# Second queue for the late loads, a new emission order and float32 for the first pairs, in a fused linear-attention and feed-forward kernel

## The chip, the cores and the metric

The kernel runs on one core of one Trainium2 chip. The metric is the device time of one execution in microseconds, median of several runs; the profile is of one such execution. TensorE is called PE in the rows, VectorE DVE, ScalarE ACT, GpSimd POOL, and the queue of SyncE, which issues the transfers, SP or SPq.

## The reference

```python
def phi(x):                                       # S1, S2: (8, 32)
    a = np.einsum('rd,bhsd->bhsr', S1, x)
    b = np.einsum('rd,bhsd->bhsr', S2, x)
    return np.einsum('bhsi,bhsj->bhsij', a, b).reshape(*x.shape[:-1], 64)
q_p, k_p = phi(q), phi(k)                         # q, k, v: (4, 4, 1088, 32)
kv = np.einsum('bhsf,bhsd->bhfd', k_p, v)
z = np.sum(k_p, axis=2)
num = np.einsum('bhsf,bhfd->bhsd', q_p, kv)
den = np.einsum('bhsf,bhf->bhs', q_p, z)[..., None] + 1e-06
x = (num / den).transpose(0, 2, 1, 3).reshape(4352, 128)
h = np.maximum(x @ w_in, 0.0)                     # w_in: (128, 2048)
out = (s * (h * h) + b) @ w_out                   # w_out: (2048, 128)
```

## The kernel before, in words

The 4352 tokens are cut into nine tiles: tile 0 has 256 of them, tiles 1 to 8 have 512. A batch is 1088 tokens, so a tile may need the attention states of two batches. `kvphase(b)` builds the state of one batch: `load_k` and `load_v` bring K and V in three groups of 128-row chunks, `kgroup` makes the features (matmuls L219, a copy `bk` on ACT, two products `ph` on DVE), L249 accumulates them with V, and L272 spreads the sums into `kv_st[b]` with the selection matrix, which lies in the small constant tile `cst_sb`. `first_features` and `first_attend` then make the attention output `x0` of tile 0; `qfeatures(t)` and `qattend(t)` make that of the others, in which the features are spread over the partitions by eight small transfers (`pq`, `br`, L385 and L389) and the denominators by five more (`dc`, `rd`, `rr`).

The feed-forward part goes by eight pairs of 128 hidden columns for each tile (`first_ffn` for tile 0, `ffn` for the others): a first product into `hp`, Relu and Square on ACT, and a second product that accumulates into `ops`. For speed at float32 precision nearly all products are three fp32r matmuls: an operand is cut into a high part (a cast to fp32r, `xh`, `uh`, `wih`, `woh`) and a low part (a subtraction on DVE, `xl`, `ul`, `wil`, `wol`), and high by low, low by high and high by high are added. `product` (L502) issues the three. The weights arrive as 64-bit numbers in eight pieces of 512 KB, `Lw0` to `Lw7`; piece 2i+k is quarter i of `w_in` (k = 0) or of `w_out` (k = 1). `split_weights` makes of a piece the float32 tile `w24` (two steps on ACT, `wc_m` L133 and L149, and two on DVE, L152 and L136), then its high and low parts. Quarter i serves pairs 2i and 2i+1.

Every part is a generator, and the string `ORDER` names, step by step, which one goes on. That fixes the order of instructions within each engine's queue; an engine runs its queue strictly in that order, and each instruction waits for the data and the buffers that it needs. `ON_DVE` lists which casts and copies go to DVE rather than to ACT (the second letter group is tile and pair: `u42` is `uh` of tile 4, pair 2). `SPLIT_0` lists the pairs of tile 0 whose first product, and those whose second product, go by three fp32r matmuls; the others use one float32 matmul with `w24` and the unsplit operand. Buffers are rotated: five for K tiles, five for V tiles, three for queries, four for each of the two kinds of raw weights (the first kind also for the split queries). All transfers are issued from SP. `keep_warm` (z in `ORDER`) is a matmul on constants without a reader.

Of the kernel before, what the change touches and what calls it, by code (L numbers as in the profile page):

```python
# [61 lines left out]
def attn_ffn_kernel(ctx: ExitStack, tc: tile.TileContext, qT, kT, vp, s64, cst, w_in, w_out, outT):  # L62
    nc = tc.nc
# [21 lines left out]

    k_in, v_in = {}, {}

    def load_k(b):
        for g in groups[b]:
            kt = p5.tile([P, GROUP * P], F32, name="kt")  # L90
            nc.sync.dma_start(out=kt[:, :len(g) * P], in_=kT[:, g[0] * P:(g[-1] + 1) * P])  # L91
# [19 lines left out]
    def load_weights(i, k):  # L111
        c = slice(i * CW, (i + 1) * CW)
        raw = p4.tile([P, 2 * CW], I32, name=f"raw{k}")
        nc.sync.dma_start(out=raw, in_=(w_in, w_out)[k][:, c].bitcast(I32))
# [40 lines left out]
    def copy(key, out, in_):  # L155
        (nc.vector.tensor_copy if key in ON_DVE else nc.scalar.copy)(out=out, in_=in_)  # L156

# [131 lines left out]
    def split_x(t, x):  # L289
        N = tiles[t][1] - tiles[t][0]  # L290
        xh = p2.tile([P, NMAX], F32R, name="xh")
        xl = p2.tile([P, NMAX], F32R, name="xl")
# [2 lines left out]
        nc.vector.tensor_tensor(out=xl[:, :N], in0=x[:, :N], in1=f32(xh[:, :N]), op=ALU.subtract)  # L295
# [195 lines left out]
    def split_u(key, u, N):  # L491
        uh = p3.tile([P, 2, NMAX], F32R, name="uh")
        copy(key, uh[:, :, :N], u[:, :, :N])
        yield
# [1 line left out]
        nc.vector.tensor_tensor(out=ul[:, :, :N], in0=u[:, :, :N], in1=f32(uh[:, :, :N]), op=ALU.subtract)  # L496
# [161 lines left out]
```

## Time and profile before

| | |
|---|---|
| median of 3 runs | 251.34 us (250.73, 251.34, 253.22) |
| time of the profiled execution | 250.91 us |
| its span, first to last instruction | 248.7 us |
| PE busy | 237.7 us (96%) |
| ACT busy | 201.9 us (81%) |
| DVE busy | 193.2 us (78%) |
| POOL busy | 1.5 us (1%) |
| moved by DMA | 24.55 MB, 24.30 MB of it on one queue |

A busy PE is not PE at its peak, since the ends of its matmuls are modelled and overlap the next one. The starts are exact, so distances from start to start tell what a matmul costs. Rows of the timeline read: start, duration, engine, line, operation, output and inputs, partitions by elements, count, and in brackets how long the engine had been idle and what ended that.

### The profile page before, as it was taken

The page shows a single profiled execution, that of the slowest core. Times are in us where ns is not written, and L with a number is a line of the kernel's source. Part 1 is how long each engine was busy: PE and PEld are TensorE (multiplying, and loading weights), DVE is VectorE, ACT ScalarE, POOL GpSimd, SP SyncE. Part 2 cuts the span into 40 slices and gives each one's busy share as a digit, 9 for nine tenths or more (in the row PEclk, how much of TensorE's full clock was granted, in tenths as well). Part 3 has the DMA queues.
Part 4 walks back from the last instruction along what each step waited for, and adds up shares of the span by engine and source line. Part 5 has one row for each costly group of instructions (what it writes and reads, how often), then busy time and mean ns, then how long its engine had stood idle before and what let it go on. Part 6 is the DMA issues. An engine that isn't in the chain of part 4 may idle for free.

```text
span 248.7 us, 3985 instructions
## 1 busy us (share of the span) xinstructions
PE 237.7 (96%) x1481; PEld 194.2 (78%) x1482; DVE 193.2 (78%) x269; ACT 201.9 (81%) x266; POOL 1.5 (1%) x10
## 2 busy tenths in 40 slices
...
GB/s 214 346 401 214 205 271 146 224 173 140 146 124 32 211 14 0 143 119 71 100 43 43 108 108 0 0 45 17 69 1 0 17 72 43 0 0 3 42 0 43
DMA packets 16259, 24.55 MB, mean 99 GB/s; under 512 B 4336, under 2 KB 8176, under 8 KB 16240
## 3 DMA queue, kind: packets, MB, share of 16 engines
q1 hardware_dynamic: 16240, 24.30, 33.8%
...
## 4 chain that ended last, share of the span: by engine, by line
PE 89%; DMA 4%; SPq 4%; ACT 1%; issue 1%; DVE 1%; ACTq 0%
PE hp L502 37%; PE ops L502 36%; PE psa L416 4%; DMA raw<-w_in 2%; PE ops L249 2%; PE psa L376 2%; PE psa L502 2%; DMA kt<-kT 2%; SPq L389 2%; PE hp L306 1%; PE psa L219 1%; PE psa L272 1%; SPq L91 1%; SPq L105 1%; PE hp L592 0%
## 5 line engine op out<-in xcount | busy, mean ns | idle before, releaser
L496 DVE TENSOR_TENSOR ul<-u,uh 128x1024 fp32r<-128x1024 f32 (+1 forms) x72 | 83.4, 1162 | 13.0 <-ACT uh L156 11.8
L486 ACT ACTIVATE u<-hp 128x1024 f32<-128x1024 f32 (+1 forms) x72 | 70.3, 976 | 21.5 <-PE hp L502 12.4
L488 ACT ACTIVATE u<-u 128x1024 f32<-128x1024 f32 (+1 forms) x72 | 72.7, 1014 | 1.7
L502 PE MATMUL hp<-xh,wil 128*128 128x512 f32 (+1 forms) x144 | 56.4, 392 | 0.6 <-ACT xh L156 0.6
L502 PE MATMUL hp<-xl,wih 128*128 128x512 f32 (+1 forms) x144 | 55.5, 385 | 0.2 <-DVE xl L295 0.2
L502 PE MATMUL hp<-xh,wih 128*128 128x512 f32 (+1 forms) x144 | 55.2, 384 | 0.0
L502 PE MATMUL ops<-uh,wol 128*128 128x512 f32 (+2 forms) x144 | 53.8, 374 | 0.4 <-ACT kr L156 0.4
L502 PE MATMUL ops<-ul,woh 128*128 128x512 f32 (+2 forms) x144 | 53.4, 371 | 0.0
L502 PE MATMUL ops<-uh,woh 128*128 128x512 f32 (+2 forms) x144 | 53.2, 370 | 0.0
L156 DVE CAST uh<-u 128x1024 fp32r<-128x1024 f32 x43 | 29.7, 691 | 24.3 <-ACT u L488 17.5
L502 PEld LDWEIGHTS hp<-xh,wil 128*128 128x128 f32 x144 | 27.3, 190 | 7.0 <-ACT xh L156 0.7
L502 PEld LDWEIGHTS hp<-xl,wih 128*128 128x128 f32 x144 | 27.4, 190 | 6.1 <-DVE xl L295 0.4
L502 PEld LDWEIGHTS hp<-xh,wih 128*128 128x128 f32 x144 | 27.4, 190 | 5.8
L502 PEld LDWEIGHTS ops<-uh,wol 128*128 128x128 f32 x144 | 27.1, 188 | 5.9 <-ACT kr L156 0.6
L502 PEld LDWEIGHTS ops<-ul,woh 128*128 128x128 f32 x144 | 27.1, 188 | 5.3
L502 PEld LDWEIGHTS ops<-uh,woh 128*128 128x128 f32 x144 | 27.1, 188 | 5.0
L156 ACT CAST uh<-u 128x1024 fp32r<-128x1024 f32 (+1 forms) x29 | 27.0, 933 | 4.2 <-PE ops L502 3.6
L229 DVE TENSOR_TENSOR ph<-psa,bk 128x384 f32<-128x384 f32 x24 | 12.7, 551 | 3.2 <-ACT bk L156 3.1
L219 PE MATMUL psa<-sk,kt 128*64 128x64 f32 x144 | 7.3, 248 | 5.2 <-DVE sk L136 4.3
L219 PEld LDWEIGHTS psa<-sk,kt 128*64 128x64 f32 x144 | 6.1, 159 | 7.1 <-DVE sk L136 5.2
L133 ACT ACTIVATE wc_m<-raw 128x512 f32<-128x512 f32 x8 | 5.4, 673 | 7.4 <-DMA raw<-w_in 4.0
L249 PE MATMUL ops<-ph,vt 128*33 128x64 f32 x288 | 10.9, 229 | 0.5 <-DMA vt<-vp 0.5
...
## 6 DMA issues: line engine op xcount, KB each, us to landing
...
kt<-kT SPq DMA_DIRECT2D x12, 192.0 KB
raw<-w_in SPq DMA_DIRECT2D x4, 512.0 KB
raw<-w_out SPq DMA_DIRECT2D x4, 512.0 KB
...
```

The lines of the kernel that those rows point to most:

```text
L133: nc.scalar.activation(out=out, in_=high.bitcast(F32), func=AF.Abs, scale=2.0 ** -112)
L156: (nc.vector.tensor_copy if key in ON_DVE else nc.scalar.copy)(out=out, in_=in_)
L219: nc.tensor.matmul(av[h:h + 64, :, i, :], kt[:, i * P + h:i * P + h + 64], sk.rearrange("p (w x) -> p w x", w=2), start=(i == 0), stop=(i ...
L229: nc.vector.tensor_tensor(out=ph[:, :n, :, :, j, :].rearrange("p c a i x -> p (c a) i x"), in0=a[:, :n * 32].rearrange("p (g y) -> p g y", ...
L249: nc.tensor.matmul(kvp[0][j * 64:j * 64 + VW, p * 64:(p + 1) * 64].rearrange("q (i x) -> q i x", i=R), v_in[g0][:, l, 2 * p + j], ph[:, l, ...
L376: nc.tensor.matmul(ab[:, :N], w, x[:, :N], start=(i == 0), stop=(i == len(terms) - 1))
L389: nc.sync.dma_start(out=br[d:d + m, p, :N], in_=abs_[32 + 48 * p:32 + 48 * p + m, :N])
L416: nc.tensor.matmul(ps[:, e0:e1], w[:, p, :], x[:, p, e0:e1], start=(i == 0), stop=(i == len(terms) - 1), skip_group_check=True)
L486: nc.scalar.activation(out=u[:, :, :N], in_=hp[:, :, :N], func=AF.Relu)
L488: nc.scalar.activation(out=u[:, :, :N], in_=u[:, :, :N], func=AF.Square)
L496: nc.vector.tensor_tensor(out=ul[:, :, :N], in0=u[:, :, :N], in1=f32(uh[:, :, :N]), op=ALU.subtract)
L502: nc.tensor.matmul(out, w, x, start=(first and k == 0), stop=(last and k == len(terms) - 1))
```

## The change

Four things change together. `load_k` and `load_v` of batches 2 and 3, `load_q` from tile 3 on, and the last two weight pieces (quarter 3) are issued from GpSimd's queue instead of SP's. `ORDER` is another string. `SPLIT_0` leaves pairs 0 and 1 of tile 0 with a float32 first product, and pairs 0 to 3 with a float32 second product. `ON_DVE` has another choice of casts and copies.

```diff
-ORDER = """z z Lw0 Ls w0 s s Lk0 Lq0 k0 w0 Lk1 Lk0 k0 sqs k0 Lv0 w0 Lw1 ...
+ORDER = """Lq0 Lk0 Ls s Lk1 z s z k0 k0 k0 Lk0 Lv0 k0 k0 Lv0 Lk0 Lw2 Lw1 ...
-SPLIT_0 = (tuple(range(8)), tuple(range(8)))
-ON_DVE = """r01 t2 w0 w4 w5 x1 u10 u11 u12 u13 u14 u15 n21 x2 u22 u23 u24 ...
+SPLIT_0 = ((2, 3, 4, 5, 6, 7), (4, 5, 6, 7))
+ON_DVE = """r00 w1 w3 w5 w7 u04 x1 u10 u12 u13 u14 u15 u16 n21 x2 u20 u21 ...
...
+    def loader(late):
+
+        return nc.gpsimd if late else nc.sync
+
     def load_k(b):
-            nc.sync.dma_start(out=kt[:, :len(g) * P], in_=kT[:, g[0] * P:(g[-1] + 1) * P])
+            loader(b >= 2).dma_start(out=kt[:, :len(g) * P], in_=kT[:, g[0] * P:(g[-1] + 1) * P])
     def load_v(b):
-            nc.sync.dma_start(out=vt[:, :len(g)], in_=vp[:, g[0]:g[-1] + 1])
+            loader(b >= 2).dma_start(out=vt[:, :len(g)], in_=vp[:, g[0]:g[-1] + 1])
     def load_q(t):
-        nc.sync.dma_start(out=q[:, :n1 - n0], in_=qT[:, n0:n1])
+        loader(t >= 3).dma_start(out=q[:, :n1 - n0], in_=qT[:, n0:n1])
     def load_weights(i, k):
-        nc.sync.dma_start(out=raw, in_=(w_in, w_out)[k][:, c].bitcast(I32))
+        loader(i == 3).dma_start(out=raw, in_=(w_in, w_out)[k][:, c].bitcast(I32))
```

Lines behind `loader` stand four further down in the changed file (L502 becomes L506). Three places show what moves.

The first is the beginning of SP's queue, which issues the loads. Before:

```order
L114 DMA raw_121<-w_in 128x1024
L119 DMA s_raw<-s 128x128
L91 DMA kt<-kT 128x384
L105 DMA qt<-qT 128x256
L91 DMA kt<-kT 128x384 x2
L98 DMA vt<-vp 128x396
L114 DMA raw_164<-w_out 128x1024
L91 DMA kt<-kT 128x384
L98 DMA vt<-vp 128x396 x2
L114 DMA raw_195<-w_out 128x1024
L105 DMA qt<-qT 128x512
L123 DMA cst_sb<-cst 128x322
```

Now:

```order
L109 DMA qt<-qT 128x256
L95 DMA kt<-kT 128x384
L123 DMA s_raw<-s 128x128
L95 DMA kt<-kT 128x384 x2
L102 DMA vt<-vp 128x396 x2
L95 DMA kt<-kT 128x384
L118 DMA raw_169<-w_in 128x1024
L118 DMA raw_171<-w_out 128x1024
L109 DMA qt<-qT 128x512
L102 DMA vt<-vp 128x396 x2
L118 DMA raw_221<-w_in 128x1024
L127 DMA cst_sb<-cst 128x322
```

Queries, K, `s` and V have moved ahead of the weights. The first weights are now quarter 1 of `w_in` (raw_169) and quarter 0 of `w_out` (raw_171), and quarter 0 of `w_in` (raw_221) stands just ahead of the constants.

The second is GpSimd's queue behind its four small copies, where nothing stood before. Now:

```order
L95 DMA kt<-kT 128x384
L118 DMA raw_417<-w_in 128x1024
L95 DMA kt<-kT 128x384
L109 DMA qt<-qT 128x512
L118 DMA raw_456<-w_out 128x1024
L95 DMA kt<-kT 128x384
L102 DMA vt<-vp 128x396 x3
L95 DMA kt<-kT 128x384 x2
L109 DMA qt<-qT 128x512 x2
```

The first of these transfers waits for the first K tile's buffer (its L223 matmuls), the second and the fifth for no buffer at all, the third for the second K tile's buffer, the fourth for the first query buffer (the L310 matmuls).

The third is PE's queue around the first feed-forward product of tile 0 (`hp` with 256 columns). Before:

```order
L344 MATMUL psa<-pq,kv_94 128x256 x2
L219 MATMUL psa<-sk,kt 64x2x32 x6
L592 LDWEIGHTS const-bfloat16-1.0
L592 MATMUL hp<-const-bfloat16-1.0 128x512
L352 MATMUL psa<-cst_sb,rx 128x128 x2
L219 MATMUL psa<-sk,kt 64x2x32 x6
L502 MATMUL hp<-xh,wil 128x256
L502 MATMUL hp<-xl,wih 128x256
```

Now:

```order
L348 MATMUL psa<-pq,kv_94 128x256 x2
L356 MATMUL psa<-cst_sb,rx 128x128 x2
L596 LDWEIGHTS const-bfloat16-1.0
L596 MATMUL hp<-const-bfloat16-1.0 128x512
L253 MATMUL ops<-ph,vt 33x64 x12
L223 MATMUL psa<-sk,kt 64x2x32 x6
L506 MATMUL hp<-x_326,w_00_107 128x256 x4
L223 MATMUL psa<-sk,kt 64x2x32 x6
```

The first product now takes `x0` itself and the float32 weights, four matmuls for two pairs; one group of L219 has moved from ahead of it to behind it.

More of the change, by code (lines that the diff above doesn't have):

```diff
@@ L30 @@
 EPS = 1e-6
-ORDER = """z z Lw0 Ls w0 s s Lk0 Lq0 k0 w0 Lk1 Lk0 k0 sqs k0 Lv0 w0 Lw1 Lk0 k0 k0 k0 p Lv0 Lv0 w1 k0 k0 sqs Lw5 k0 w1 w0 k0 w0 w1 k0 k0 k1 w5 k0 Lq1 k1 Lcst w1 k0 k0 Lw2 k1 p Lv1 w5 Lk1 q1 Lk2 k0 k0 k1 w5 q1 k0 k1 p w0 Lw4 k0 w2 f w5 Lv1 f w2 Lq2 w1 w2 f f w2 f Lw3 k1 f k1 w2 w4 z f k1 Lk1 k1 q1 q1 w4 f w2 f q1 q1 f w3 k2 00 w4 k2 q1 q1 q1 k2 w4 k1 w3 00 k1 00 k2 02 q2 w3 k1 k1 00 02 02 q1 00 03 01 k1 Lk2 Lq3 q1 Lk2 n1 q2 Lk2 03 03 w4 Lv1 w3 02 n1 Lw6 n1 k2 03 n1 q3 k1 w4 k2 w6 k1 k1 05 02 w1 00 03 k2 01 Lw7 n1 q3 k2 n1 Lk2 k2 q2 w5 w6 01 04 k1 q2 w3 w6 k2 n1 k2 04 n1 w3 w6 01 q2 q2 01 02 n1 03 q2 04 q2 w6 01 05 k2 k1 04 w6 q3 q2 k2 06 w5 07 q2 04 05 05 06 k2 06 q3 05 n1 w7 q2 04 w7 n1 05 n2 k1 Lk2 Lk3 n2 n2 06 Lq4 k2 n1 Lq8 n1 q3 Lk3 n1 k3 w7 n1 q3 06 w7 Lk3 07 n2 10 07 k3 q4 Lq6 n2 k2 12 w7 07 q8 w7 q3 q4 10 q3 06 11 k2 q4 10 07 n2 07 12 10 10 q3 q3 12 10 12 12 Lq5 13 11 Lk3 q3 k3 11 13 q3 11 11 16 12 k3 13 n2 n2 16 13 n2 13 q3 11 q5 15 16 Lk3 q3 q3 14 q4 k1 15 13 q5 n3 q6 n2 n2 15 q4 16 n2 07 15 n3 17 q4 16 Lk3 14 n3 n3 15 q4 k2 q4 n3 14 n3 q4 k2 n2 n2 k3 k2 q4 n3 k3 17 16 n3 q5 q4 k3 17 15 17 n2 q4 q8 14 n3 14 20 17 q4 q5 07 n3 q4 q4 20 q5 k2 21 14 q5 17 21 q6 23 n3 q5 k3 k3 20 21 24 Lq7 n4 20 20 17 n3 21 k3 k3 q5 23 k3 20 q5 21 23 24 22 26 n3 n3 24 23 q5 n4 23 21 24 22 k3 22 k3 n4 n3 q5 q5 k3 24 26 q6 22 25 q6 q7 q5 23 n4 22 26 26 q7 24 25 k3 q5 25 30 q5 25 22 26 q6 30 n5 n4 k3 n4 27 q6 q6 33 k3 30 n5 q6 25 n5 q6 27 n4 30 27 n4 30 26 n4 k0 27 27 35 33 n5 33 25 33 q6 n4 35 k3 30 35 q6 27 n5 33 32 k3 34 q6 q7 32 n4 31 n4 q6 17 q6 35 q6 q7 n5 q7 35 32 q7 32 k3 33 32 n5 n6 q7 q7 34 q7 34 34 n5 36 31 q8 31 35 n5 n4 34 n6 37 q7 31 n4 34 31 q7 32 36 n4 37 q7 40 n5 36 36 37 36 n6 q8 27 n5 37 n6 40 q7 31 n5 40 n6 36 37 40 41 n5 41 n6 41 27 37 40 41 n5 42 41 q7 42 q7 44 43 q8 n6 42 44 40 n7 42 44 n6 42 q8 37 45 44 43 n5 44 41 43 43 43 q8 46 42 q8 45 44 q8 n7 q8 50 n6 45 45 46 45 46 q8 n7 43 50 q8 50 47 45 46 46 47 56 50 n6 47 50 47 56 46 56 56 47 q8 q8 56 50 n6 52 52 54 47 q8 n8 52 n7 52 51 54 n6 n7 52 54 52 51 54 55 51 54 n6 n7 55 37 55 56 51 n7 n6 53 n7 54 57 55 51 55 51 n8 47 53 55 n7 n6 60 57 53 57 53 57 n8 63 53 60 60 n7 57 63 47 63 53 n7 57 n8 60 62 60 64 63 63 62 65 62 64 60 62 62 64 n7 64 n8 61 n7 n8 65 63 64 65 65 n7 66 61 n8 65 61 62 66 67 61 57 n7 66 61 67 64 n8 70 65 66 67 61 66 67 74 70 n8 66 67 72 70 74 n8 57 70 74 70 n8 72 72 67 74 71 74 73 70 n8 67 72 74 71 72 71 73 71 n8 73 73 76 71 75 n8 76 n8 73 72 76 67 75 76 71 75 77 80 76 75 77 77 73 75 77 77 80 76 80 81 81 75 80 77 83 84 81 81 80 80 83 83 81 84 85 83 84 81 77 82 83 84 84 85 85 82 83 86 85 82 85 77 86 82 82 86 87 84 87 85 86 86 87 87 82 86 87 87 87 87 87 87 87 z z z z z"""
@@ new lines @@
+ORDER = """Lq0 Lk0 Ls s Lk1 z s z k0 k0 k0 Lk0 Lv0 k0 k0 Lv0 Lk0 Lw2 Lw1 w2 p Lq1 k0 k0 Lv0 k0 w2 k0 Lv1 sqs w2 k1 k0 k0 w1 w1 p k0 k1 Lw0 k0 k0 Lcst k0 Lv1 w2 Lw4 k1 k0 sqs k1 Lq2 q1 k0 Lk1 w0 p Lk2 q1 k0 k0 Lw5 w0 w1 z Lw3 f f f f w0 f f w4 f z w0 f k1 k1 w1 w4 w2 k1 w5 w4 w1 k1 f q1 k1 w5 00 01 q1 w4 w5 00 q1 q1 q1 k2 q1 01 01 w2 q2 w4 00 q1 q1 k1 f k2 Lw6 k2 03 Lk2 w3 Lk1 Lq3 00 k2 w3 q2 01 w0 q1 Lv1 02 Lw7 w0 Lk2 03 w6 n1 w3 w4 n1 w3 03 Lk2 n1 n1 k1 w5 n1 n1 k1 w6 k1 02 k1 04 02 w6 03 04 w5 k1 q2 w6 q3 q3 q2 02 05 k1 q2 k1 k2 w3 w6 Lk2 04 n1 k2 q2 k1 w7 n1 n1 w6 04 05 q2 k2 q2 05 w5 07 k2 k2 q2 06 w7 k1 05 q2 q3 04 w3 w7 n1 05 07 n1 07 k2 k2 q2 04 k2 Lk2 k2 05 Lk3 k2 07 q3 n2 n1 n1 n2 06 Lk3 n2 k2 n1 q3 k1 n1 k3 06 06 07 w7 10 n2 Lq4 w7 12 06 10 n2 w7 q3 10 q3 w1 k3 11 q4 n2 k3 12 06 07 10 12 07 Lq6 k2 q3 10 q4 n2 11 q3 13 q3 10 q3 11 q3 n2 Lk3 12 n2 16 Lq5 12 Lk3 n2 11 12 13 q3 q3 q4 13 11 q3 q6 q4 16 k2 15 k3 11 k1 q4 13 n2 n3 n3 n2 13 16 16 15 n3 q5 17 q4 13 k2 16 n3 k3 q6 15 17 q4 n2 k0 k2 k3 Lk3 n2 14 n3 15 16 15 n2 n3 q5 17 n3 q4 k2 20 k3 14 17 k3 14 q5 q4 15 k3 q4 q4 17 20 k2 14 21 Lq8 n3 20 14 20 n3 22 20 21 14 Lk3 21 q4 q4 q4 22 q4 q5 17 21 n3 22 07 21 24 26 q5 q5 q5 22 22 q8 17 n4 k3 24 k3 20 k3 23 Lq7 n4 k3 24 q5 26 n4 24 k3 q7 q5 n4 q8 n3 q5 n4 q5 26 24 k3 21 23 n4 26 n3 23 22 n3 q5 26 23 25 n3 24 q5 26 n3 25 q5 k3 n4 q6 23 27 k3 q5 q6 27 23 q6 q6 25 k3 27 25 q6 q7 n5 25 30 q6 n4 q6 35 k3 27 q6 q6 30 k3 27 30 25 n5 30 31 35 35 n4 35 k3 n4 q6 30 33 q7 n4 27 31 q6 35 34 17 30 31 31 n4 33 n5 33 q7 35 q6 31 33 33 q6 32 34 31 n5 q7 34 q7 32 34 37 n5 32 n4 q7 33 q7 36 34 n4 36 n6 q7 q8 n4 32 n5 32 34 36 32 q7 n6 37 40 37 36 37 n5 36 n6 41 40 40 q7 36 37 n5 42 q7 n6 27 41 40 40 37 q7 41 q8 44 41 41 n6 n6 n5 n5 q7 42 n6 44 q7 43 q8 n5 42 40 44 q8 41 q8 n5 n6 42 42 q8 44 27 n7 43 45 43 42 44 43 45 n7 45 n5 q8 n5 47 n7 43 45 45 q8 n6 n5 47 44 46 q8 n7 n6 47 47 47 q8 n6 46 43 46 50 46 50 n6 q8 52 46 50 52 52 37 37 45 50 50 56 46 47 q8 51 50 n7 52 56 q8 56 52 n7 n8 52 56 55 51 51 56 n7 51 54 55 n7 51 55 n8 56 54 55 n6 54 55 n8 54 53 n6 n7 n6 51 53 54 57 53 53 63 53 57 55 54 63 57 60 n7 64 53 57 n8 63 57 63 60 60 47 63 n8 60 57 n8 n7 60 66 64 64 60 64 64 66 62 n8 n7 66 63 65 62 66 62 66 64 n7 62 65 n7 62 61 66 47 65 61 67 65 57 65 n8 n7 61 67 n8 61 62 70 n8 67 67 61 70 65 71 67 74 70 61 67 70 71 71 70 57 72 74 71 74 76 n8 71 72 70 75 74 71 74 72 n8 76 72 73 72 76 74 75 76 72 76 n8 75 73 73 77 75 76 n8 75 77 67 n8 73 80 81 75 73 77 73 77 80 83 77 80 80 81 81 80 81 77 86 81 83 83 83 83 67 85 86 80 86 85 84 85 86 86 77 84 81 82 85 85 84 82 83 84 84 87 86 85 77 82 84 87 87 82 82 87 87 82 87 87 87 87 z z 87 z 87 z z z"""
```

2 lines of the change are left out of this document (1 added, 1 removed).

## The prediction

> **What bounds the kernel now.** I read the busy line of the page first, then busy time by stage, then the timeline at the places where a stage is not full.
>
> ```profile
> PE 237.7 (96%) x1481; PEld 194.2 (78%) x1482; DVE 193.2 (78%) x269; ACT 201.9 (81%) x266; POOL 1.5 (1%) x10
> ```
>
> ```profile
> 0.00:4.00 4.00, 1.01 (x2) 0.14 (x2) 0.00 (x0) 1.28 (x1) 0.76 (x6) 1.00 0.49 144
> 4.00:8.00 4.00, 1.80 (x25) 1.50 (x25) 1.52 (x6) 2.37 (x8) 0.71 (x4) 1.00 1.01 333
> 8.00:12.00 4.00, 4.00 (x43) 3.18 (x43) 3.34 (x8) 1.73 (x4) 0.00 (x0) 1.00 1.00 354
> 12.00:16.00 4.00, 3.27 (x72) 2.19 (x67) 3.25 (x7) 2.58 (x6) 0.00 (x0) 1.00 1.06 402
> 16.00:20.00 4.00, 3.61 (x61) 3.08 (x63) 3.96 (x11) 2.83 (x6) 0.00 (x0) 1.00 0.94 362
> 20.00:24.00 4.00, 2.40 (x25) 1.77 (x26) 3.92 (x9) 3.39 (x9) 0.00 (x0) 0.98 0.79 185
> 24.00:28.00 4.00, 4.00 (x45) 3.61 (x45) 3.56 (x7) 2.52 (x6) 0.00 (x0) 0.59 0.69 187
> 28.00:32.00 4.00, 4.00 (x39) 2.55 (x39) 3.92 (x8) 3.94 (x10) 0.00 (x0) 1.00 0.84 239
> 32.00:36.00 4.00, 3.15 (x58) 2.73 (x53) 2.22 (x5) 2.50 (x8) 0.00 (x0) 1.00 0.88 296
> 60.00:228.00 168.00, 168.00 (x816) 136.33 (x815) 133.05 (x166) 142.26 (x157) 0.00 (x0) 1.00 0.22 58
> ```
>
> After the window and its length the columns are PE, PE's weight loads, DVE, ACT and POOL busy, the granted clock, the DMA engines' share and GB/s. From 60 to 228 us PE is busy for 168.00 of 168.00 at clock 1.00, while the DMA engines are at 0.22. There nothing on another engine or queue can move the end, only PE work or a new hole. The first 36 us are different: the DMA engines are full from 4 to 20 us (1.01, 1.00, 1.06, 0.94), PE has holes, and 24 to 28 us runs at clock 0.59, behind a window in which PE was busy for 2.40 of 4.00. So the question is **when PE becomes full**, and how much work it then has left. I take the first feed-forward matmul of tile 0 as the mark:
>
> ```profile
> 6.06 1.95 PE L219 MATMUL psa<-sk,kt 128*64 128x64 f32 x24 [4.28 <-DVE sk L136]
> 16.21 0.68 PE L272 MATMUL psa<-cst_sb,kr 128*128 128x128 f32 x4 [0.90 <-ACT abq L156]
> 19.10 0.57 PE L219 MATMUL psa<-sk,kt 128*64 128x64 f32 x12
> 21.15 0.84 DVE L358 TENSOR_TENSOR x<-num,psa 64x256 f32<-64x256 f32 x2
> 22.48 0.38 PE L502 MATMUL hp<-xh,wil 128*128 128x256 f32 x1 [0.58 <-ACT xh L156]
> 23.10 0.39 PE L502 MATMUL hp<-xl,wih 128*128 128x256 f32 x1 [0.24 <-DVE xl L295]
> ```
>
> The mark is at 22.48 us. Behind it PE loses 0.24 us (the wait for `xl`) and 0.85 us (3.15 of 4.00 between 32 and 36), 1.1 us of idle time; and, at clock 0.59 for 4.00 busy us, 4.00 x 0.41 = 1.6 us of clock. All else to the end is work.
>
> **The change part by part.**
>
> *Float32 instead of three fp32r matmuls.* The 12 products concerned are two pairs times two column blocks for the first product and four pairs times two for the second. What each form costs from start to start:
>
> ```profile
> 42.92 0.28 PE L502 MATMUL ops<-uh,wol 128*128 128x258 f32 x1
> ...
> 44.24 0.28 PE L502 MATMUL ops<-uh,woh 128*128 128x258 f32 x1
> 44.48 1.97 PE L416 MATMUL psa<-pq,kv 128*128 128x320 f32 x8
> 46.37 0.86 PE L249 MATMUL ops<-ph,vt 128*33 128x64 f32 x24
> ```
>
> The fp32r matmuls stand 11 steps in 1.32 us, 0.12 us each, so a triple is 0.36 us. The L416 row holds four float32 matmuls, 1024 columns in all, and takes 46.37 - 44.48 = 1.89 us, 1.85 ns a column: 0.48 us for 256. Each exchange adds 0.12 us to PE, and 12 of them **1.4 us**. They could cost nothing only in a hole of PE, and all stand behind the mark, where the holes are 1.1 us in all; I count them in full. What they spare, four casts to `uh` on ACT and four subtractions on DVE (0.69 us each), and pairs 0 and 1 not waiting for `xh`, counts through the mark alone, since neither engine is the bound later.
>
> *One group of L219 behind the mark.* It costs what the 19.10 row shows, **0.5 us** from start to start, since there is one less ahead of the mark.
>
> *The mark itself.* What `sk` needs arrives earlier: `s_raw` is now behind 0.33 MB instead of 0.52 MB, and ACT works on it before any weights, so PE's start at 6.06 us should come some tenths earlier. But the path then runs into the loads. The tile of constants, without which L272 can't run, stands behind 3.79 MB of SP's queue (it and all ahead of it), against 3.59 MB before. How such a place turns into time:
>
> ```profile
> 10.43 0.69 ACT L133 ACTIVATE wc_m<-raw 128x512 f32<-128x512 f32 x1 [2.13 <-DMA raw<-w_out]
> 13.21 0.68 ACT L133 ACTIVATE wc_m<-raw 128x512 f32<-128x512 f32 x1 [1.30 <-DMA raw<-w_out]
> kt<-kT SPq DMA_DIRECT2D x12, 192.0 KB
> raw<-w_in SPq DMA_DIRECT2D x4, 512.0 KB
> ```
>
> Both ACT rows waited for a load and nothing else. The first load ends 2.04 MB down the queue, the second 3.16 MB. The GB/s of the windows add up to 0.58, 1.91, 3.33, 4.93 and 6.38 MB at 4, 8, 12, 16 and 20 us; they pass 2.04 MB at 8.4 us and 3.16 MB at 11.5 us. So a load lands 1.7 to 2.1 us behind that curve; I take 1.9.
>
> With SP's queue alone, 3.79 MB is passed at 13.1 us and the constants land at 15.0. ACT, which takes two weight pieces ahead of the `kr` copy, is ready by then, and L272 starts behind the L380 matmul, at about 15.4 us. From L272 to the mark it was 22.48 - 16.21 = 6.3 us; the cast of `xh` (0.45 us behind the end of `x0` at 21.99) no longer lies in it, and two `ph` products no longer stand just ahead of `x0` on DVE (0.6 us). That leaves 5.2 us and the **early bound of the mark, 20.6 us**.
>
> Now GpSimd's queue. "Late" loads are not late there: nothing else stands in that queue, so they go as soon as their buffers are free. The first five (192 + 512 + 192 + 256 + 512 KB, 1.70 MB) need the first two L219 groups and L306 done, or nothing:
>
> ```profile
> 7.94 3.09 PE L306 MATMUL hp<-qt,srep 128*128 128x256 f32 x8
> 24.64 0.58 SPq L91 DMA_DIRECT2D kt<-kT  x1
> 27.99 0.43 SPq L114 DMA_DIRECT2D raw<-w_in  x1
> 28.46 0.43 SPq L114 DMA_DIRECT2D raw<-w_out  x1
> ```
>
> Before, SP issued the last weights at 27.99 and 28.46 us. Now they go out between about 7 and 12 us, into DMA engines that are full until 20. If all 1.70 MB passes ahead of the constants, those end at 5.49 MB, 17.5 us on the curve, and land at 19.4; L272 runs at once, and the mark is at 19.4 + 5.2 = 24.6 us, the **late bound**. No run here shows two queues sharing the engines, so I take the middle of 20.6 and 24.6: **22.6 us, +0.1** against before.
>
> The Trainium skill bears on this ("DMA: Bandwidth & Descriptors", sections "Issuing engines are not separate DMA queues" and "Queues, rings and completion order"): transfers of all issuing engines run on the same 16 DMA engines, which serve the queues in turn, so a second queue saves issue time alone. The full shares from 4 to 20 us agree that there is no spare engine; by that rule alone the sum would be the first rival's, 255.6 us.
>
> *Idle time and clock behind the mark.* The hole between 32 and 36 us ended with V and weights that SP had issued at 27 to 28.5 us; these weights now come early, so I let 1.1 us of idle time become 0.7, **-0.4**. It can't fall by more than 1.1. The clock I leave: PE's queue still holds a chain of waits ahead of the mark, as between 20 and 24 us before. A gain there is bounded by 1.6 us, a loss by as much again.
>
> *SP's queue and the tail.* SP gives up 18 issues of 0.4 to 0.6 us each. What hides that is PE, full from 36 us on. `q` and `n` transfers come sooner; nobody waits for them. In the tail the last `uh` moves from DVE to ACT:
>
> ```profile
> 239.65 0.28 PE L502 MATMUL ops<-uh,wol 128*128 128x256 f32 x1
> 240.64 1.22 DVE L496 TENSOR_TENSOR ul<-u,uh 128x1024 fp32r<-128x1024 f32 x1
> 241.01 0.28 PE L502 MATMUL ops<-uh,wol 128*128 128x256 f32 x1
> 241.79 0.68 DVE L156 CAST uh<-u 128x1024 fp32r<-128x1024 f32 x1
> ```
>
> That cast waited for DVE's subtraction of the pair before; on ACT it needn't, but is some 0.2 us slower. PE has 1.36 us of work for each pair (239.65 to 241.01) to cover it: 0, with 0.3 us either way.
>
> *The sum.* +0.1 (mark) + 1.4 (float32) + 0.5 (L219 group) - 0.4 (idle) = +1.6 us. On the profiled execution (250.91 us: a span of 248.7 and 2.2 around it) this gives 252.5. The median of the runs shown is 0.43 us higher, so I predict **252.9 us**.
>
> **The rivals.** *GpSimd's queue takes its full share* (slower): the place is the constants and quarter 0 of `w_in`, the price 2.1 us at the mark (24.6), 1.4 and 0.5 us as above, and some 0.3 us of clock, since PE starves longer ahead of the mark: +4.3, 255.6 us. It decides as soon as about 1.7 MB from GpSimd is moved before SP's 3.79 MB; GpSimd is idle from 8 us on in the windows, which speaks for it. Against it: no row says how soon GpSimd's transfers start after their issue.
>
> *The loads don't collide* (GpSimd's start late or move slowly): the mark at 20.6, -1.9 + 1.9 - 0.4 = -0.4, 250.9 us. The Trainium skill names a cause ("SBUF — State Buffer", "Who interferes with whom"): DVE's casts from SBUF to SBUF can block GpSimd while it makes its descriptors. Few casts stand in DVE's queue ahead of the mark, which speaks against it; later, each such cast is short:
>
> ```profile
> L156 DVE CAST uh<-u 128x1024 fp32r<-128x1024 f32 x43 | 29.7, 691 | 24.3 <-ACT u L488 17.5
> ```
>
> At 0.69 us a cast a load of K, V or queries would come a little later, and none is waited for in the full part of PE.
>
> *No collision, and PE no longer starves* (faster): the same, and PE is kept so full that the clock stays at 1.00 and no hole is left, which takes off 1.1 + 1.6 us where the case above took 0.4: -2.7 us, 248.6. Against it: PE's queue still holds L330, L348 and L356 with an engine's answer between each.
>
> *The new order starves PE in the full part* (60 to 228 us), by ACT's longer list of casts: ACT has 168.00 - 142.26 = 25.7 us free there and DVE 35, so I give it little; 2 us more than the forecast, 254.9.
>
> **How the numbers follow.** A difference under 1% (2.5 us, 248.8 to 253.9) is about what a measurement of this kernel can't tell from no change. The forecast (251.6 to 254.2) has a chance of 0.40, full sharing (254.2 to 257) 0.25, no collision (249.5 to 251.6) 0.22, no collision and no hole 0.10, starving 0.03. Slower: 0.25 + 0.03 and 0.05 of the forecast's upper end, 0.33. Faster: 0.10, and 0.01 for what no case holds. The same: 0.56. For 8 in 10 the range takes in the early and the late mark with the clock's uncertainty above, and leaves out most of the case without holes: 249.0 to 256.6 us.
>
> **What would show it.** Right: L223 starts before 6 us; GB/s still near 400 from 8 to 16 us, but with a second queue in the table of queues; L276 waits for the constants; the mark at 22 to 23 us; PE full from there on, the clock low once. Wrong: the mark under 21.5 us with PE full behind it, or waits of PE after 60 us, or a float32 product that costs PE far from 0.48 us. If L276 runs at 19 us or later, the sharing rival is right.

## The result and the profile after

The changed kernel takes 260.88 us (median; 258.76 to 261.98), the kernel before 251.34 in the same runs: a ratio of 1.038, 95% interval 1.0338 to 1.0422. Slower by 9.5 us, where 1.6 were forecast and 256.6 was the range's end. The profiled execution took 260.73 us, its span is 258.6 us, 9.9 more than before. Here and below medians are of all executions, while the ratios leave out one disturbed execution each of e1 (338 us), e10 (259 us) and e13 (822 us), and as e1's profile fell on that one, e5 is the same kernel once more.

The page of the changed kernel, its busy line and its table of queues (packets, MB, share of the engines' time):

```profile
PE 243.0 (94%) x1472; PEld 196.6 (76%) x1472; DVE 187.8 (73%) x261; ACT 202.3 (78%) x266; POOL 12.9 (5%) x30
...
q1 hardware_dynamic: 13360, 19.28, 26.5%
q0 software_dynamic: 1536, 5.02, 5.9%
```

5.02 MB now go by GpSimd's queue. PE lost its time early again. Busy time by stage, same columns as before:

```profile
...
16.00:20.00 4.00, 1.73 (x26) 0.80 (x21) 2.14 (x5) 0.31 (x2) 1.07 (x2) 1.00 1.03 392
20.00:24.00 4.00, 3.13 (x26) 2.46 (x27) 1.45 (x6) 2.14 (x4) 0.00 (x0) 0.85 1.04 394
24.00:28.00 4.00, 4.00 (x48) 3.18 (x47) 3.55 (x8) 3.23 (x8) 1.17 (x2) 0.73 0.90 264
...
32.00:36.00 4.00, 2.50 (x15) 2.08 (x13) 1.66 (x3) 1.81 (x4) 0.00 (x0) 1.00 0.81 264
36.00:60.00 24.00, 21.37 (x221) 16.94 (x222) 21.25 (x40) 16.94 (x40) 2.13 (x4) 0.93 0.45 118
60.00:228.00 168.00, 168.00 (x821) 136.41 (x820) 132.91 (x168) 144.47 (x164) 2.02 (x3) 1.00 0.23 60
```

From 60 us on PE is full, as before. But the DMA engines now stay full until 24 us (1.04 at 394 GB/s, where it was 0.79 at 185), and between 16 and 20 us PE works 1.73 of 4.00 and ACT 0.31: everything waits for loads. There are holes at 32 to 36 and between 36 and 60 us. PE's waits, and the rows of the timeline where they end:

```profile
...
PE psa L276 <- ACT wc_m L137: 2.9, 1, 2.9
PE psa L420 <- ACT abq L160: 2.2, 1, 2.2
PE psa L223 <- ACT bk L160: 2.0, 1, 2.0
PE psa L420 <- ACT wih L160: 1.9, 1, 1.9
```

```profile
17.09 0.26 ACT L160 COPY kr<-ops 33x128 f32<-33x128 f32 x1 [3.11 <-DVE kr L160]
...
19.95 0.66 ACT L137 ACTIVATE wc_m<-raw 128x512 f32<-128x512 f32 x1 [2.60 <-DMA raw<-w_in]
20.59 0.52 PEld L276 LDWEIGHTS psa<-cst_sb,kr 128*128 128x128 f32 x4 [3.70 <-issue]
20.62 0.68 PE L276 MATMUL psa<-cst_sb,kr 128*128 128x128 f32 x4 [2.90 <-ACT wc_m L137]
...
24.08 0.69 SPq L389 DMA_DIRECT2D pq<-abq  x1
...
26.80 1.99 PE L506 MATMUL hp<-x,w 128*128 128x256 f32 x8
...
27.60 2.11 SPq L393 DMA_DIRECT2D br<-abq  x3
...
35.00 0.58 ACT L160 COPY abq<-psa 128x512 f32<-128x512 f32 x1 [2.19 <-DMA vt<-vp]
36.38 1.95 PE L420 MATMUL psa<-pq,kv 128*128 128x512 f32 x4 [1.89 <-ACT wih L160]
...
44.85 2.66 SPq L393 DMA_DIRECT2D br<-abq  x3
...
50.79 0.58 ACT L160 COPY abq<-psa 128x512 f32<-128x512 f32 x1 [1.72 <-DMA rr<-rd]
52.13 2.56 PE L420 MATMUL psa<-pq,kv 128*128 128x320 f32 x8 [2.24 <-ACT abq L160]
```

The mark is at 26.80 us, 4.3 later than before. Behind it PE waits twice at L420, once for the attention of tile 1 (1.89 us) and once for that of tile 2 (2.24), and each time ACT ahead of it stood still for a transfer. The chain of waits gives them names (start, length, what):

```profile
7.67 12.27 DMA raw<-w_in
...
30.39 4.62 DMA vt<-vp
...
43.73 4.43 DMA rd<-rc
48.22 2.57 DMA rr<-rd
```

All four are on SP's queue. The weight piece that SP issued at 7.67 us took 12.27 us; `rd`, which is 8 KB, took 4.43. But a wait for several transfers gets one name, and here three names mislead, as a look at what each instruction reads and writes shows.

- L276 is put down to `wc_m`. It reads only the constants and `kr`, whose last copy ended at 17.35, and its weight load (the PEld row) begins at 20.59, ahead of the end of `wc_m` at 20.61. It **waited for the constants**, the next load in SP's queue behind that weight piece. The last of their completion signals in the trace is at 20.49 us, 0.10 ahead of the weight load; that distance is 0.10 in e6, e7 and e11 below as well, and in e7 the profile names the constants (`PE psa L276 <- DMA cst_sb<-cst: 1.1, 1, 1.1`).
- The copies `abq` at 35.00 and 50.79 are put down to a V tile and to `rr`, which they don't touch. They overwrite what the eight transfers `pq` and `br` of the tile before read. The last of these eight was issued as the third of the `br` of the rows at 27.60 and 44.85, and its last signal is at 34.67 and 50.72. So tile 1's eight took from 24.08 to 34.67 us.

### The profile page after: what moved, and what is told of

Read it like the earlier page. It is cut to its first block, busy times and chain, and to the rows that moved or that the text cites. A ratio compares the mean times of both kernels' runs of the same rounds, so it can differ in the third digit from the quotient of the medians.

```text
span 258.6 us, 3981 instructions
## 1 busy us (share of the span) xinstructions
PE 243.0 (94%) x1472; PEld 196.6 (76%) x1472; DVE 187.8 (73%) x261; ACT 202.3 (78%) x266; POOL 12.9 (5%) x30
## 3 DMA queue, kind: packets, MB, share of 16 engines
q0 software_dynamic: 1536, 5.02, 5.9%
## 4 chain that ended last, share of the span: by engine, by line
PE 81%; DMA 9%; SPq 5%; ACT 2%; issue 1%; DVE 1%
PE hp L506 35%; PE ops L506 33%; PE psa L420 5%; DMA raw<-w_in 5%; PE psa L506 2%; DMA vt<-vp 2%; DMA rd<-rc 2%; SPq L393 2%; PE ops L253 1%; PE psa L380 1%; DMA rr<-rd 1%; SPq L102 1%; SPq L95 1%; PE psa L348 1%; PE psa L276 1%
## 5 line engine op out<-in xcount | busy, mean ns | idle before, releaser
L500 DVE TENSOR_TENSOR ul<-u,uh 128x1024 fp32r<-128x1024 f32 (+1 forms) x68 | 80.9, 1190 | 21.5 <-ACT uh L160 20.3
L506 PE MATMUL hp<-xh,wil 128*128 128x512 f32 (+1 forms) x140 | 55.0, 393 | 0.0
L506 PE MATMUL hp<-xl,wih 128*128 128x512 f32 (+1 forms) x140 | 54.0, 385 | 0.0
L506 PE MATMUL hp<-xh,wih 128*128 128x512 f32 (+1 forms) x140 | 54.0, 385 | 0.0
L506 PE MATMUL ops<-uh,wol 128*128 128x512 f32 (+2 forms) x136 | 51.4, 378 | 0.0
L506 PE MATMUL ops<-ul,woh 128*128 128x512 f32 (+2 forms) x136 | 51.0, 375 | 0.0
L506 PE MATMUL ops<-uh,woh 128*128 128x512 f32 (+2 forms) x136 | 51.0, 375 | 0.0
L160 DVE CAST uh<-u 128x1024 fp32r<-128x1024 f32 (+1 forms) x42 | 28.7, 683 | 17.9 <-ACT u L492 14.2
L506 PEld LDWEIGHTS hp<-xh,wil 128*128 128x128 f32 x140 | 26.4, 189 | 6.1 <-ACT u L490 0.3
L506 PEld LDWEIGHTS hp<-xh,wih 128*128 128x128 f32 x140 | 26.3, 188 | 5.7
L506 PEld LDWEIGHTS hp<-xl,wih 128*128 128x128 f32 x140 | 26.4, 188 | 5.6 <-DVE xl L299 0.2
L506 PEld LDWEIGHTS ops<-uh,wol 128*128 128x128 f32 x136 | 25.5, 188 | 5.5
L506 PEld LDWEIGHTS ops<-ul,woh 128*128 128x128 f32 x136 | 25.6, 188 | 5.2
L506 PEld LDWEIGHTS ops<-uh,woh 128*128 128x128 f32 x136 | 25.6, 188 | 5.1
L395 DVE TENSOR_TENSOR pq<-pq,br 128x1024 f32<-128x1024 f32 x8 | 9.8, 1220 | 4.8 <-DMA vt<-vp 2.3
L253 PEld LDWEIGHTS ops<-ph,vt 128*33 128x33 f32 x288 | 10.9, 133 | 3.0 <-issue 1.2
L223 PE MATMUL psa<-sk,kt 128*64 128x64 f32 x144 | 7.8, 255 | 5.2 <-DVE sk L140 3.1
L253 PE MATMUL ops<-ph,vt 128*33 128x64 f32 x288 | 12.5, 251 | 0.0
```

The lines of the kernel that those rows point to most:

```text
L223: nc.tensor.matmul(av[h:h + 64, :, i, :], kt[:, i * P + h:i * P + h + 64], sk.rearrange("p (w x) -> p w x", w=2), start=(i == 0), stop=(i ...
L253: nc.tensor.matmul(kvp[0][j * 64:j * 64 + VW, p * 64:(p + 1) * 64].rearrange("q (i x) -> q i x", i=R), v_in[g0][:, l, 2 * p + j], ph[:, l, ...
L395: nc.vector.tensor_tensor(out=pq[:, :, :N], in0=pq[:, :, :N], in1=br[:, :, :N], op=ALU.mult)
L506: nc.tensor.matmul(out, w, x, start=(first and k == 0), stop=(last and k == len(terms) - 1))
```

## The experiments

Thirteen runs. "All on SP" is the changed kernel with `loader` returning `nc.sync`. The table has the medians, the ratio to the kernel before as it ran beside each (250.65 to 251.34 us), L276 (L272 before) and the mark in us, and PE's waits at L420 for tile 1 and tile 2.

| kernel | us | ratio, 95% interval | L276 | mark | waits |
|---|---|---|---|---|---|
| before | 251.34 | | 16.21 | 22.48 | 0, 0 |
| changed | 260.88 | 1.038 (1.0338 to 1.0422) | 20.62 | 26.80 | 1.9, 2.2 |
| e1, e5: all on SP | 251.24 | 1.0004 (0.9972 to 1.0036) | 17.00 | 21.79 | 0, 0.3 |
| e2: before, late loads on GpSimd | 257.86 | 1.0246 (1.0181 to 1.0311) | 16.20 | 22.48 | 2.5 at tile 1 |
| e3: before, float32 in all first products of tile 0 | 251.45 | 1.0018 (0.9985 to 1.0052) | | 22.11 | 0.4 at tile 1 |
| e4: changed, gated by `x0` | 258.86 | 1.0315 (1.0256 to 1.0374) | 16.55 | 21.35 | 4.9, 1.7 |
| e6: weights alone on GpSimd | 252.48 | 1.0065 (1.0044 to 1.0086) | 18.87 | 23.64 | 0.3, 0.8 |
| e7: K, V, queries alone | 258.62 | 1.0323 (1.0269 to 1.0377) | 17.25 | 23.46 | 2.9, 2.1 |
| e8: urgent ones on GpSimd | 258.34 | 1.0326 (1.0277 to 1.0374) | 15.79 | 20.59 | 5.6, 0.9 |
| e9: the same, SP held | 255.26 | 1.0149 (1.01 to 1.0198) | 16.54 | 21.32 | 0, 2.9 |
| e10: changed, gated by `br` of tile 1 | 255.30 | 1.0141 (1.0085 to 1.0198) | 17.99 | 22.77 | 0.3, 2.8 |
| e11: all on SP, weights ahead | 252.43 | 1.0047 (1.0023 to 1.0071) | 18.66 | 23.43 | 0, 0.4 |
| e12: constants alone on GpSimd | 250.88 | 0.9986 (0.9963 to 1.0009) | 16.51 | 21.28 | 0.4, 0.7 |
| e13: changed, held at tiles 1 and 2 | 253.03 | 1.0088 (1.0062 to 1.0113) | 16.32 | 21.10 | 0.3, 0 |

### The queue, or the rest of the change? (e1, e2, e3, e5)

e1 takes the queue away and leaves the order, float32 and casts; e2 puts the queue alone into the kernel before; e3 puts float32 alone into it.

```diff
 # e1, e5
-        return nc.gpsimd if late else nc.sync
+        return nc.sync
 # e2: before.py, with loader() in load_k, load_v, load_q, load_weights as in the change
 # e3: before.py
-SPLIT_0 = (tuple(range(8)), tuple(range(8)))
+SPLIT_0 = ((), tuple(range(8)))
```

> The changed kernel, but every load is issued from SP again (the new order, the float32 pairs and the new choice of engines stay). Theory of the shared DMA engines: GpSimd's early loads delayed the constants and quarter 0 of w_in, so without them L276 starts at 15.4 to 17 us instead of 20.62, the first feed-forward matmul at 20.5 to 23 us instead of 26.80, and the time is 249 to 253 us. Rival, the new order itself: the loads of SP only come in another sequence, L276 stays near 20 us or PE keeps its holes between 34 and 53 us, and the time stays at 258 us or more.

> The kernel before, with nothing changed but the issuing queue: the same late loads go by GpSimd. Theory of the shared DMA engines: they are issued as soon as their buffers are free, L272 and the first feed-forward matmul (16.21 and 22.48 us before) come 1 to 4 us later, and the time is 252 to 257 us. In this order GpSimd's two weight pieces stand behind a V tile, whose buffer is freed later than in the changed kernel, so less than in the changed kernel. Rival, the new order itself: the queue alone changes nothing, 250.5 to 252 us.

> The kernel before, with the first product of all eight pairs of tile 0 as one float32 matmul instead of three fp32r ones: 16 exchanges. By the prediction's price of 0.12 us each, PE has 1.9 us more to do and the time is 253 us or a little less, since the first ones no longer wait for xh and the weights' parts. If float32 costs nothing, 251 us; if it is a main part of the change's loss, 255 us or more.

> The changed kernel with every load back on SP's queue (order, float32 products and casts as changed), once more, for a trace. If the second queue alone makes the loss: about 251 us, L276 at 15 to 17 us without a wait for a weight piece, the mark at 20.6 to 22 us, no wait of PE for abq above 1 us and no hole of more than 1 us behind the mark. If instead the new order itself had holes that the all-SP time hides by a gain elsewhere: the waits of L420 for abq (2.2 and 1.9 us in the changed kernel) are still there.

All on SP the changed kernel is where the kernel before is, 1.0004. The queue alone costs 2.5% in the old order. So the loss is the queue's. Rows of e5 (250.62 us):

```profile
17.00 0.68 PE L276 MATMUL psa<-cst_sb,kr 128*128 128x128 f32 x4
19.94 0.69 SPq L389 DMA_DIRECT2D pq<-abq  x1
21.79 1.99 PE L506 MATMUL hp<-x,w 128*128 128x256 f32 x8
23.71 0.57 PE L223 MATMUL psa<-sk,kt 128*64 128x64 f32 x12
25.45 0.58 SPq L118 DMA_DIRECT2D raw<-w_in  x1
27.32 1.90 PE L506 MATMUL ops<-u,w 128*128 128x258 f32 x8
28.66 0.59 ACT L160 COPY abq<-psa 128x512 f32<-128x512 f32 x1 [0.78 <-DMA raw<-w_in]
28.87 0.47 PE L506 MATMUL hp<-xh,wil 128*128 128x256 f32 x1
29.18 0.28 PE L506 MATMUL hp<-xl,wih 128*128 128x256 f32 x1
```

L276 waits for nothing, and the mark is 5.0 us earlier than in the changed kernel. In e2 the mark does not move, where I had expected it 1 to 4 us later: GpSimd issued its second load there at 12.86 us, when the constants had been issued 5 us before. The loss is all behind the mark. The two issues, and e2's waits of PE:

```profile
7.49 0.67 SPq L127 DMA_DIRECT2D cst_sb<-cst  x1
...
12.86 0.54 POOL L95 DMA_DIRECT2D kt<-kT  x1 [4.69 <-PE psa L223]
```

```profile
PE psa L223 <- DMA kt<-kT: 3.2, 1, 3.2
PE psa L420 <- DVE pq L395: 2.5, 1, 2.5
```

### Which bytes hurt where? (e4, e6, e7, e11)

e6 leaves only the two weight pieces on GpSimd, e7 only K, V and queries. e11 has no second queue: these weight pieces stand on SP, ahead of the constants. e4 keeps all late loads on GpSimd but holds them until `x0` is there.

```diff
 # e6: loader(False) for K, V and queries; e7: loader(False) for the weights
 # e11: all on SP, and in ORDER
-... Lcst ... Lw6 ... Lw7 ...
+... Lw6 Lw7 Lcst ...
 # e4, in load_weights (gate is a tile of its own)
+        if (i, k) == (3, 0):
+            nc.gpsimd.tensor_copy(out=gate, in_=x_first[0][:, :1])
```

> The changed kernel, with one small copy on GpSimd ahead of its second load that reads x0: the late loads still go by GpSimd, but only from the end of the first attention on (about 20 us) instead of from 6.8 us. Theory of the shared DMA engines: until then SP has the engines nearly alone, L276 starts at 15.5 to 17 us, the first feed-forward matmul at 20.5 to 23 us, and the time is 249 to 253 us. Rival, GpSimd's transfers are slow or disturb DVE as such: 256 us or more. Rival, the new order itself: 258 us or more.

> The changed kernel with only the two last weight pieces (1.02 MB) on GpSimd's queue; K, V and queries all on SP. Sharing by bytes: 1.02 of the 1.70 MB that went ahead of the constants are left, so L276 comes at 18 to 19 us instead of 20.6 and the mark at 23.5 to 24.5; fewer bytes stand against the feature transfers of tiles 1 and 2, so idle time behind the mark is 1 to 2 us: 253 to 255 us. Rival, that only the mark or only the feature chains are hurt by one class of loads: if the weights are harmless, 251 us; if they make all of it, 260 us.

> The changed kernel with only K and V of batches 2 and 3 and the late queries on GpSimd's queue; all weights on SP. Sharing by bytes: 0.64 MB ahead of the constants instead of 1.70, so L276 at 17 to 18 us and the mark at 22 to 23; six or more K and V loads run against the transfers pq and br of tile 1, so PE waits 1.5 to 3 us there: 254 to 256 us. If losses add up, this run's loss and that of the weights alone together give some 9 us. Rival: software-made descriptors are slow as such, then this run, with most of the transfers on GpSimd, is as slow as the changed kernel, 259 to 261 us.

> Every load on SP, in the changed order, with the two last weight pieces (1.02 MB) moved in that order to just ahead of the constants. No second queue. Theory, that bytes which go ahead are what counts and not the queue they are on: L276 at 18.5 to 19.5 us, the mark at 23.3 to 24.3, little idle time behind it, 252 to 253.5 us, as with these pieces on GpSimd. Rival, that GpSimd's queue itself costs something: the mark under 22.5, 251 us or less.

L276 of e6, then of e11 (the marks are in the table):

```profile
18.87 0.68 PE L276 MATMUL psa<-cst_sb,kr 128*128 128x128 f32 x4 [0.71 <-DVE pq L316]
```

```profile
18.66 0.68 PE L276 MATMUL psa<-cst_sb,kr 128*128 128x128 f32 x4 [0.73 <-DVE pq L316]
```

The two pieces, 1.05 MB (the expectations have 1.02), do to the mark on GpSimd's queue what they do on SP's own queue ahead of the constants: 23.64 and 23.43, and 252.48 and 252.43 us. So for the mark it is the **bytes that go ahead** that count, not the queue. But the mark is the smaller part. e6 and e7 have their marks 0.2 us apart, and e7 is 6.1 us slower: K, V and queries go on being issued while the transfers of tiles 1 and 2 run, and PE waits 2.9 and 2.1 us there. e4 shows the same from the other side: its mark, 21.35, is no later than that of all on SP, and nearly the whole loss stays, since the loads that it held back meet the transfers of tile 1 (4.9 us). Its 258.86 us, where I had expected 249 to 253, is in the range of both its rivals; e1 rules out the new order, and e6 beside e11 and e9 below speak against a GpSimd that is slow or disturbs DVE as such. I had expected e7 at 254 to 256 us, too low by 2.6, and e6 at 253 to 255, too high by 0.5.

### Is GpSimd's queue slow, or do loads run ahead? (e8, e9)

In e8 all loads are on SP; GpSimd issues the constants and, for tiles 1 and 2, the thirteen transfers of each. They are small one by one, beside weight pieces of 512 KB; but the eight `pq` and `br` of a tile (two of 256 KB, four of 96, two of 64) together move 1.05 MB, as much as two weight pieces. e9 adds a transfer on SP that must wait for the first half of `br`, so that SP's later loads wait too.

```diff
 # e8: all loads on SP, but cst_sb on nc.gpsimd, and for pq, br, dc, rd, rr
+    def loader2(t):
+        return nc.gpsimd if t <= 2 else nc.sync
 # e9: e8, and in qfeatures behind the transfers of each half p
+            if t <= 2 and p == 0:
+                hold = dr.tile([1, 32], F32, name="hold")
+                nc.sync.dma_start(out=hold, in_=br[96:97, 0, :32])
```

> The roles turned round: all loads on SP, and on GpSimd only what is small and urgent, the constants (165 KB) and the thirteen feature and denominator transfers of tiles 1 and 2. If a queue's share of the engines is what counts, the small ones no longer stand behind loads: the constants land before 8 us, L276 waits for nothing but its input (15 to 16 us), the mark 20.5 to 21.5, no hole at the features of tiles 1 and 2; 249.5 to 251 us, not slower than with everything on SP. Rival: GpSimd's transfers are slow as such (descriptors made in software, some us each): thirteen transfers in a chain come 1 to 2 us later each, PE waits for pq at L420, and the time is 253 to 256 us.

> The reversed roles of the run before (constants and the transfers of tiles 1 and 2 on GpSimd, loads on SP), and SP held back as in the one-queue kernel: a small transfer on SP reads the first half of br of tiles 1 and 2, so SP issues no further loads until that half has landed. Theory, that loads which run ahead are what delays the feature transfers: mark at 20.5 to 21, the eight transfers of tile 1 take 8 us or less from first issue to last landing, no wait of PE for wih or abq above 1 us, 249.5 to 251.5 us. Rival, that GpSimd's transfers are slow as such: PE still waits 2 us or more at the features of tiles 1 and 2, 254 us or more.

With the constants early the mark of e8 came at 20.59. But a queue of their own did not make the small transfers quick. The copy `abq` of tile 2 can't run until those of tile 1 have read `abq`; e8, then e9:

```profile
15.10 0.33 SPq L122 DMA_DIRECT2D raw<-w_in  x1
...
19.29 0.54 POOL L393 DMA_DIRECT2D pq<-abq  x1 [12.91 <-ACT num L356]
...
33.02 0.58 ACT L164 COPY abq<-psa 128x512 f32<-128x512 f32 x1 [6.03 <-DMA br<-abq]
```

```profile
20.03 0.54 POOL L393 DMA_DIRECT2D pq<-abq  x1 [13.86 <-ACT num L356]
...
24.69 0.35 SPq L122 DMA_DIRECT2D raw<-w_in  x1
...
27.92 0.58 ACT L164 COPY abq<-psa 128x512 f32<-128x512 f32 x1 [0.51 <-PE ops L513]
```

In e8 `abq` was free 13.7 us behind the first issue (19.29 to 33.02), in e9 after 7.9 (20.03 to 27.92), with no wait for them. Both issue them from GpSimd, so GpSimd's queue is not slow as such. What differs is SP: with the small transfers taken off its queue, nothing makes it wait, and it issued the seventh weight piece at 15.10 us, ahead of them; in e5 that piece follows at 25.45, behind them. **On one queue the small transfers are also a brake on the loads behind them.** So e8, expected at 249.5 to 251 us, took 258.34. In e9 the brake is back at tile 1, and the wait there is gone. At tile 2 2.9 us stay, and with 255.26 us that is what the rival of e9 had forecast. Its reason, slow transfers of GpSimd, does not fit tile 1; e9 holds SP only until the first half of `br` is there, and e13 below, which holds the loads until tile 2's second half, has no wait at tile 2.

### Held to the order of one queue (e10, e12, e13)

e10 and e13 keep the late loads on GpSimd and hold them by one-column copies on GpSimd that read `br`. e12 has the constants alone on GpSimd.

```diff
 # e10, ahead of GpSimd's second load
+            nc.gpsimd.tensor_copy(out=gate, in_=br_first[0][:, 0, :1])
 # e13, in loader: one copy once the first half of br of tile 1 is issued,
 # one once the second half of that of tile 2 is (br_first: those halves)
+            while br_first:
+                br, p = br_first.pop(0)
+                nc.gpsimd.tensor_copy(out=gate, in_=br[:, p, :1])
 # e12: all on SP, and
-        nc.sync.dma_start(out=cst_sb, in_=cst)
+        nc.gpsimd.dma_start(out=cst_sb, in_=cst)
```

> The changed kernel, late loads on GpSimd, with a one-column copy on GpSimd ahead of its second load that reads br of tile 1, so all but 192 KB of the late loads go only when those transfers have landed (24.5 to 28.5 us). Theory of loads that run ahead: the mark at 21.5 to 22.5, tile 1's transfers as with one queue, no hole at 34 us; the weight pieces come up to 3 us late, which ACT may wait for; 251 to 254 us. Rival, that a second queue costs wherever it is busy: as with the earlier gate, 256 to 259 us.

> Every load on SP in the changed order but the constants (161 KB), which go by GpSimd's queue. They landed with 12.9 us there before, so L276 waits only for its input: 15.5 to 16 us, the mark 20.5 to 21.1, about 1 us earlier than with everything on SP; the features of tile 1 still on SP, so no new hole; 249.3 to 250.4 us, 0.2 to 0.6 per cent below the kernel before. Rival: the weights of quarter 0, SP's loads still, hold the path next, or SP's loads run ahead by the time of one issue: no gain, 250.6 us.

> The changed kernel, late loads on GpSimd, held at two places by one-column copies on GpSimd: all but its first load until the first half of tile 1's br has landed, and those behind the second V tile of batch 2 until the second half of tile 2's br has landed. That is about where SP would have issued them. Theory, that the whole loss comes from loads which run ahead of the constants and of the transfers of tiles 1 and 2: the mark at 21.8 to 22.8 us, no wait of PE for abq above 1 us at 34 or 47 us, clock once low at most, 250.8 to 252.5 us. Rival, that a second queue keeps a cost of its own beside the collisions: the wait at tile 2 (2.8 us with one gate) stays, and the time is 254 us or more.

Each hold takes away the wait at its place. e10 has 0.3 us left at tile 1 and 2.8 at tile 2, e13 0.3 and none, and its mark is at 21.10. By its ratio (1.0088) e13 is 2.2 us above the kernel before, where the changed kernel is 9.5 above, with the same loads on the same queue. That is still more than the 250.8 to 252.5 us that I expected. Most of what is left stands at tile 3, where nothing holds: between 56 and 64 us PE is busy for 3.54 and 2.74 of each 4.00. From the chain of waits of e13, and rows of its timeline:

```profile
48.12 7.01 DMA dc<-nd
```

```profile
49.97 3.23 SPq L399 DMA_DIRECT2D br<-abq  x3
...
59.44 1.23 DVE L403 TENSOR_TENSOR pq<-pq,br 128x1024 f32<-128x1024 f32 x1 [2.01 <-DMA rd<-rc]
...
63.95 0.47 PE L428 MATMUL psa<-pqh,kvl 128*128 128x512 f32 x1 [0.66 <-DVE kvl L292]
```

The 4 KB of `dc` took 7.01 us, just behind the loads that the second hold had kept (GpSimd issued nine from 42.84 us on), and DVE stood for it. Then DVE stood for L403, which reads `pq` and `br` of tile 3, and not `rd`; the last signal of that `br` is at 59.12 us. So I take running ahead for the cause of nearly all of the loss; that tile 3 is again this cause fits the rows, but no run held the loads there. e10 was expected at 251 to 254 us and took 255.30. e12 brought the mark forward by 0.5 us and gained no measurable time (0.9963 to 1.0009); 249.3 to 250.4 us were expected. No version tried is faster than the kernel before by more than its interval.

## Why the prediction was wrong, point by point

**What bounds the kernel** held: in the changed kernel too PE is full from 60 to 228 us (168.00 of 168.00), and the difference arises before.

**The mark** was the first wrong term and the largest: +4.3 instead of +0.1. The step that failed is "I take the middle". The prediction itself noted that nothing else stands in GpSimd's queue and that GpSimd is idle; that spoke for the late bound, and e11 beside e6 shows that the bytes then count in full. But the late bound, 24.6, fell short as well, by 2.2. Its mechanism was right: L276 waited for the constants, one of the prediction's own signs. They landed at 20.49 us instead of 19.4: when their last packet was through, at 19.91 us, the packets of the trace add up to 1.90 MB of GpSimd's queue and 4.18 of SP's, where the prediction counted 1.70 and 3.79. From L276 at 20.62 it was then 6.2 us to the mark, not 5.2, since PE ran at a lower clock for part of it (0.85 and 0.73 in the windows); with the clock at 1.00 e5 needs 21.79 - 17.00 = 4.8. The early bound, 20.6 with SP's queue alone, was 1.2 too early: e5 has 21.79. L276 started there at 17.00 instead of 15.4, behind L380 as forecast, which ended only at 16.90, and the path behind it was 0.4 shorter. That e8's mark, 20.59, meets this bound is luck, since its constants go by GpSimd; with them alone there (e12) it is 21.28.

What the Trainium skill says in "DMA: Bandwidth & Descriptors" ("Issuing engines are not separate DMA queues"), that all issuers share the same 16 engines, agrees with e6 and e11. That a second queue saves issue time alone is too mild for this case: it costs 1.038 times the time.

**The idle time behind the mark** was the second wrong term, and its sign was wrong too: -0.4 was written, about +3.0 measured (1.9 + 2.2 at the two L420 rows, against 1.1 before). I counted the earlier weights as a gain, and priced the collision at one place, the constants. It recurs wherever a chain of small transfers stands that PE waits for: tile 1 and tile 2 here, tile 3 in e13. The first rival, full sharing, had the right mechanism, and L276 at 20.62 is past the 19 us that the prediction named as its sign. Its 255.6 fell short since it was priced at one place instead of three, and 2.2 us too low there. The rival of loads that don't collide is out: L276 came 3.6 us later than with all on SP, and e9's small transfers, made by GpSimd, were as quick as SP's (7.9 us, against 8.7 in e5 from the first issue to `abq`).

**Float32** held. A first product costs (23.71 - 21.79)/4 = 0.48 us in e5, as worked out. Behind four second products the next matmul starts at 28.87, but from it to the one at 29.18 it is 0.31 us, where others take 0.12; with these 0.19 the four cost (28.87 + 0.19 - 27.32)/4 = 0.44 each. The other four, reckoned in the same way, cost 0.97 for each two. All twelve cost 5.6 us, against 12 x 0.36 = 4.3: **1.3** instead of 1.4.

e3 has 16 exchanges of first products, which should cost 1.9, and its ratio of 1.0018 is only 0.45 us (0.9985 to 1.0052). Two windows of its trace say why:

```profile
24.00:28.00 4.00, 3.97 (x28) 2.74 (x24) 4.00 (x8) 3.82 (x10) 0.00 (x0) 1.00 0.69 186
28.00:32.00 4.00, 2.28 (x6) 0.68 (x4) 4.00 (x8) 3.12 (x7) 0.00 (x0) 1.00 0.91 279
```

The low clock of before (0.59 at 24 to 28 us) is absent, 1.6 us back, and a hole has come in at 28 to 32. Behind the mark PE waits 2.4 us instead of 1.1, the mark is 0.4 earlier, and the span is 1.1 longer (249.8 us). So 1.1 + 1.6 + 0.4 - 1.3 = 1.8 are left for the exchanges. Terms of this size hide one another in a median; only the starts of the rows separate them.

**The clock** behind the mark was right by chance: 0.93 over 24 us is 1.7 us, against 1.6 before, but at another place. **One L219 group** (0.5) is behind the mark, as said. **SP's queue and the tail** show no wait of PE (SP gave up 20 issues, not 18: POOL has 30 instructions on the page instead of 10).

The sum that should have stood there: 4.3 + 3.0 + 1.3 + 0.5 + 0.1 = 9.2 of the 9.9 us. The other 0.7 I can't place. All on SP the same sum gives -0.7 (mark) - 0.4 (idle) + 1.3 + 0.5 - 1.6 (clock) = -0.9, and the span is 0.1 longer, so some 1.0 us seem to belong to the new order or casts, not to the queue; no run divides them.
